# An added zero matmul and copy, and three stores, ahead of the reads of a flag at the end of a one-core attention and maxout kernel

## The chip, the cores and the metric

The kernel runs on one core of a Trainium2 chip. The metric is the device time of one execution in microseconds (us). The five engines of the core (TensorE, VectorE, ScalarE, GpSimd, SyncE) have an instruction stream each and wait for one another through semaphores. In the profile they are PE (with PEld for the loading of weights), DVE, ACT, POOL and SP; a "q" behind the name (SPq, ACTq, DVEq, PEldq) marks instructions that the engine's sequencer handles, such as the issue of a DMA, the load of a register or a branch.

## What is computed

```
scores  = x @ state^T / sqrt(64)           x 8 x 8 x 512 x 64, state 8 x 8 x 32 x 64
xread   = softmax(scores) @ state
sread   = softmax(state @ x^T / sqrt(64)) @ x
y       = concat([xread, sread])           per batch 544 rows of 512 features
h       = max(y @ w1, y @ w2, y @ w3)      512 -> 768
out     = h @ w_out                        768 -> 512, 4352 rows, float32
```

Softmax in the reference subtracts the maximum of each row. The kernel first computes everything without that subtraction and looks at the sums of the exponentials. If all are within bounds, the result stands. If not, everything is computed again with the maximum subtracted.

## The kernel before

The order of the work on every engine is written out by hand, as a list of short words that the kernel performs in turn: FIRST for the batches 0 to 2 and the loading, EACH for a batch in the middle, LAST for batch 7 and for the states' rows of all batches ("s"). Each word is a function in a table: `l2p b j c0 c1` computes columns c0 to c1 of the rows j of a batch's output into a PSUM bank (six accumulating matmuls, line 460), `l2pc` copies that piece to SBUF on the engine named by its last letter (line 464; D for VectorE, A for ScalarE), `sop` stores it from the queue named (line 470, or 468 for rows of the states; S for SyncE, A for ScalarE, P for GpSimd). `l2`, `l2c` and `so` do the same for whole rows of 512 columns (lines 445, 452, 475), `sos` stores a whole row of the states' output (line 483).

PSUM is held as four banks and two pairs of banks. The string BANKS lists, for each bank that the plan asks for in turn, which of the four it gets. The last eight entries before the change are, for the last eight pieces, 2 0 3 1 2 3 0 1; the last of them, bank 1, belongs to `l2p 7 0 128 256`, which VectorE copies and ScalarE stores. The entry before it in the same bank is `l2p s 0 0 256`, which ScalarE copies.

`busy n` (keep_busy) sends n matmuls of a tile of zeros into a bank that nobody reads. FIRST uses it at the start.

The sums are looked at by `look` (VectorE) and turned into a single integer, the flag, by `flag`: one matmul, a reduction and a comparison, lines 502 to 505. `vl` (read_flag, line 510) lets every engine load the flag from SBUF into a register of its own. Each engine then compares the register and branches (line 600): if the flag is zero it jumps over the block that computes everything again. The branch is hinted as likely taken. After the block every engine sets its semaphore to the value that it would have with the block, and SyncE goes through a list of final waits, for all DMA queues and all engines, before the barrier that ends the program. The profile gives these last steps to line 665, that of the call of the kernel.

As every engine's stream is in the order of the words, `vl` stands on each engine behind the work that the list names ahead of it and before what it names later. Before the change `vl` has three words behind it, which are all SyncE's: `sos 1 S`, `sop s 0 0 256 S` and `sop 7 0 256 384 S`. On TensorE and VectorE it is behind the last matmul and the last copy, on ScalarE behind the last store, on GpSimd behind its own last store.

Of the kernel before, what the change touches and what calls it, by code (L numbers as in the profile page):

```python
# [9 lines left out]
F32 = mybir.dt.float32  # L10
BF16 = mybir.dt.bfloat16
# [46 lines left out]
    l2pc 7 3 0 256 D; l2pc s 0 256 512 D; sop s 0 256 512 A; l2pc 7 2 0 128 A; l2p 7 1 128 384;  # L58
    sop 7 2 0 128 A; l2p 7 0 256 384; l2p 7 1 384 512; l2pc s 0 0 256 A; l2p 7 0 128 256;
    l2pc 7 1 128 384 A; l2c s 1 D; sop 7 3 0 256 S; sop 7 2 128 384 P; l2pc 7 0 256 384 D;  # L60
    sop 7 1 128 384 A; l2pc 7 1 384 512 D; sop 7 1 384 512 A; l2pc 7 0 128 256 D; sop 7 0 128 256 A; vl;
    sos 1 S; sop s 0 0 256 S; sop 7 0 256 384 S;
"""

BANKS = """
# [3 lines left out]
"""  # L69
PAIRS = """  # L70
    0110101010 1010101010 1001010010 1001010010 10
# [4 lines left out]
def kernel(  # L76
# [10 lines left out]
    nc = tc.nc  # L87

    B, H, S, D = x.shape
# [16 lines left out]
    work = ctx.enter_context(tc.tile_pool(name="work", bufs=2))  # L106
# [18 lines left out]
    zero = const.tile([128, 512], BF16, name="zero")  # L125
# [17 lines left out]
    def bank(shape, dtype, name):  # L143
        return pp.tile(shape, dtype, tag="b" + next(homes["b"]), bufs=1, name=name)
# [364 lines left out]
    def read_flag():  # L509
# [3 lines left out]

    table = {
        "lst": (load_st, 0), "lx": (load_x, 1), "lxg": (load_x_heads, 1), "lxu": (load_x_uncast, 1),
        "cxu": (cast_x, 1), "lw": (load_w, 0), "lwo": (load_wout, 0), "zero": (set_zero, 0),
# [6 lines left out]
        "gr": (g_run, 1), "grc": (g_ran, 1), "l1": (layer1, 1), "l1s": (layer1_states, 0),  # L525
        "m0": (max_first, 1), "ma": (max_second, 1), "mb": (max_third, 1), "l2": (layer2, 1), "l2c": (layer2_out, 1),
        "l2p": (layer2_part, 1), "l2pc": (layer2_part_out, 1), "sop": (store_part, 1), "so": (store, 1), "sos": (store_states, 0), "look": (look_at_sums, 0), "flag": (set_flag, 0),
        "vl": (read_flag, 0),
    }

    def value(t):
# [138 lines left out]
```

## Time and profile before

| | us |
|---|---|
| median of three runs | 155.25 |
| the three runs | 154.92, 155.25, 155.26 |
| the profiled execution | 154.63 |
| its span, first to last instruction | 152.8 |
| TensorE busy in the span | 146.5 (96%) |
| VectorE busy | 114.4 (75%) |
| ScalarE busy | 85.1 (56%) |
| GpSimd busy | 54.0 (35%) |

The profiled execution's mean granted TensorE clock is 0.994 of full speed. Its own time holds 1.8 us beside the span. Times inside the trace count from the start of the span.

The rows shown below are of these kinds. A row of the chain of waits, or of the timeline, has start, length, engine, line, operation and tiles, with the count of what is merged. A row for one line of the kernel has engine, operation and count, then the shortest, median and longest duration in nanoseconds, then the first and the last start in microseconds. A row of waits names who waited, for whom, and the microseconds in total, the number of waits and the longest. A row of DMA packets names the queue, the number of packets that began in the window, their megabytes, and the time that they took as a share of 16 DMA engines over the window; as a packet counts with its whole length where it began, a short window can hold more than 100%.

### The profile page before, as it was taken

The page shows a single profiled execution, that of the slowest core. Times are in us where ns is not written, and L with a number is a line of the kernel's source. Part 1 is how long each engine was busy: PE and PEld are TensorE (multiplying, and loading weights), DVE is VectorE, ACT ScalarE, POOL GpSimd, SP SyncE. Part 2 cuts the span into 40 slices and gives each one's busy share as a digit, 9 for nine tenths or more (in the row PEclk, how much of TensorE's full clock was granted, in tenths as well). Part 3 has the DMA queues.
Part 4 walks back from the last instruction along what each step waited for, and adds up shares of the span by engine and source line. Part 5 has one row for each costly group of instructions (what it writes and reads, how often), then busy time and mean ns, then how long its engine had stood idle before and what let it go on. Part 6 is the DMA issues. An engine that isn't in the chain of part 4 may idle for free.

```text
span 152.8 us, 3639 instructions
## 1 busy us (share of the span) xinstructions
PE 146.5 (96%) x1433; PEld 73.6 (48%) x1433; DVE 114.4 (75%) x201; ACT 85.1 (56%) x147; POOL 54.0 (35%) x73
## 2 busy tenths in 40 slices
PE   6899999999999999999999999999999999999970
PEld 2465444344445443544354434443444445689660
DVE  1698899889168798879887988898879878664540
ACT  0776876779677762776277627762676362522020
POOL 6978527302246506440644063407140100003300
PEclk9999999999999999999999999999999999999997
DMA  4999999992919979987398839973052300300572
GB/s 110 242 193 202 198 197 203 166 193 41 202 70 241 228 99 271 132 183 178 138 131 183 180 137 133 197 166 137 4 178 54 137 4 2 137 0 21 191 288 66
DMA packets 38053, 22.30 MB, mean 146 GB/s; under 512 B 21504, under 2 KB 35840, under 8 KB 38032
## 3 DMA queue, kind: packets, MB, share of 16 engines
q0 software_dynamic: 14672, 13.44, 45.3%
q1 hardware_dynamic: 21920, 6.95, 22.5%
q10 hardware_dynamic: 1440, 1.64, 3.3%
q8 instruction: 12, 0.20, 0.5%
q14 instruction: 9, 0.07, 0.2%
HBM read 15.20 MB, written 8.91 MB: 158 GB/s over the span
## 4 chain that ended last, share of the span: by engine, by line
PE 92%; ACT 2%; DMA 2%; DVE 1%; issue 0%; ACTq 0%
PE pw L414 47%; PE po L445 25%; PE pg L361 6%; PE po L460 4%; PE ps L260 3%; PE idle L209 2%; PE psr L325 2%; DMA stf<-in_state_dram 2%; PE pgh L361 1%; ACT L226 1%; ACT xT L242 1%; PE pat L293 1%; PE pxt L235 1%; PE pt L220 0%; ACT bd L226 0%; ACT st L215 0%
## 5 line engine op out<-in xcount | busy, mean ns | idle before, releaser
L414 PE MATMUL pw<-aT,G 128*128 128x512 bf16 x288 | 66.6, 379 | 0.0
L429 ACT CAST t<-pw 128x512 bf16<-128x512 f32 (+1 forms) x54 | 30.4, 563 | 35.2 <-PE pw L414 23.1
L414 PEld LDWEIGHTS <-G 128*128 128x128 bf16 x288 | 27.2, 98 | 33.8 <-issue 2.4
L434 DVE TENSOR_TENSOR t<-t,pw 128x512 bf16<-128x512 bf16 (+1 forms) x54 | 35.3, 654 | 10.1 <-ACT t L429 7.6
L445 PE MATMUL po<-wout,ht 128*128 128x512 bf16 x168 | 39.8, 379 | 0.0
L438 DVE TENSOR_TENSOR ht<-t,pw 128x512 bf16<-128x512 bf16 x48 | 32.9, 686 | 4.1
L445 PEld LDWEIGHTS <-ht 128*128 128x128 bf16 x168 | 15.3, 98 | 19.2 <-issue 2.1
L475 POOL DMA_DIRECT2D out_dram<-osb x12 | 6.9, 574 | 49.4 <-ACT t L429 27.2
L282 POOL TENSOR_TENSOR a<-e,rden 128x1024 bf16<-128x1024 bf16 (+1 forms) x9 | 14.8, 1647 | 11.6 <-DVE rden L276 10.5
L401 ACT CAST G<-pg 128x1024 bf16<-128x1024 f32 (+1 forms) x19 | 17.1, 908 | 0.0
L309 POOL COPY xp<-x 128x1024 bf16<-128x1024 bf16 x12 | 12.3, 1065 | 4.8 <-DMA x<-in_x_dram 4.8
L452 DVE COPY osb<-po 128x512 f32<-128x512 f32 x14 | 9.6, 685 | 5.6 <-PE po L445 5.6
L452 ACT COPY osb<-po 128x512 f32<-128x512 f32 x15 | 8.9, 593 | 5.8 <-PE po L445 5.8
L209 PE MATMUL idle<-zero 128*128 128x512 bf16 x30 | 10.2, 440 | 1.3 <-DVE zero L187 1.3
L361 PE MATMUL pg<-w,bd 64*32 64x512 bf16 (+1 forms) x288 | 10.8, 362 | 0.0
L274 DVE TENSOR_REDUCE seen<-e 128x32 f32<-128x1024 bf16 (+1 forms) x10 | 10.0, 998 | 0.5 <-ACT e L267 0.4
L267 ACT ACTIVATE e<-ps 128x1024 bf16<-128x1024 f32 (+1 forms) x10 | 8.6, 861 | 1.6 <-PE ps L260 1.5
L401 DVE CAST G<-pg 128x1024 bf16<-128x1024 f32 (+1 forms) x10 | 9.5, 948 | 0.0
L470 POOL DMA_DIRECT2D out_dram<-osb x4 | 2.1, 540 | 19.9 <-ACT osb L464 19.9
L379 ACT CAST G<-pg 128x768 bf16<-128x768 f32 (+1 forms) x10 | 7.7, 773 | 2.1 <-PE pg L361 2.1
L414 PE MATMUL pw<-atp,w 128*128 128x256 bf16 x72 | 8.7, 272 | 0.0
L414 PEld LDWEIGHTS <-w 128*128 128x128 bf16 x72 | 6.9, 98 | 1.5
(68 smaller groups left out, 112.5 us busy)
## 6 DMA issues: line engine op xcount, KB each, us to landing
out_dram<-osb POOLq DMA_DIRECT2D x11, 512.0 KB, 3.2
x<-in_x_dram POOLq DMA_DIRECT2D x4, 512.0 KB, 7.0
x<-in_x_dram POOLq DMA_DIRECT2D x7, 256.0 KB, 8.7
w<-in_moe_w_dram POOLq DMA_DIRECT2D x3, 384.0 KB, 8.8
w<-in_moe_w_dram POOLq DMA_DIRECT2D x4, 256.0 KB, 8.0
wout<-in_moe_w_out_dram POOLq DMA_DIRECT2D x1, 768.0 KB, 9.9
out_dram<-osb SPq DMA_DIRECT2D x3, 256.0 KB, 2.3
osb<-in_x_dram SPq DMA_DIRECT2D x1, 512.0 KB, 4.2
```

The lines of the kernel that those rows point to most:

```text
L209: nc.tensor.matmul(p, zero[:, 0:128], zero, start=True, stop=True)
L274: nc.vector.reduce_sum(out=den, in_=parity(e[b], g), axis=AX.X)
L282: times[c](out=parity(a[b], g).rearrange("p j g s n -> p j (g s) n"), in0=parity(e[b], g).rearrange("p j g s n -> p j (g s) n"), in1=rdens ...
L309: nc.gpsimd.tensor_copy(out=xp[b][:, :, :, g * (D + 1):g * (D + 1) + D], in_=v[:, g])
L361: nc.tensor.matmul(p(s, g), bd(b, 2 * s + g)[64 * g:64 * g + 64, g, :], f(w_sb[64 * g:64 * g + 64, s]), start=True, stop=True, tile_positi ...
L401: copier[c[g]](out=v[:, g:h], in_=p[:, g:h, 0:c1 - c0])
L414: nc.tensor.matmul(pw[i][:, 0:n], lhs(i, k), rhs(k), start=(k == 0), stop=(k == nk - 1))
L429: nc.scalar.copy(out=t0s[b, m][:, 0:n], in_=open_ps["l", b, m][0][:, 0:n])
L434: nc.vector.tensor_max(t1s[b, m][:, 0:n], t0s.pop((b, m))[:, 0:n], open_ps["l", b, m][1][:, 0:n])
L438: nc.vector.tensor_max(ht[b][:, m, :], t1s.pop((b, m))[:, 0:n], open_ps.pop(("l", b, m))[2][:, 0:n])
L445: nc.tensor.matmul(p, ht[b][:, m, j * 128:(j + 1) * 128], wout_sb[:, m, :], start=(m == 0), stop=(m == NM - 1))
L452: copier[c[i]](out=o[:, j, i * w:i * w + w], in_=p[:, i * w:i * w + w])
```

## The change

A new word, `hold`, sends one matmul of zeros (128 x 128 weights, 512 columns) to one more entry of BANKS, which is bank 1 again, and lets VectorE copy the 128 x 512 result into a new tile, `held`, which nobody reads. `vl` moves behind `hold`, to the end of LAST. So on TensorE the zero matmul stands ahead of the read of the flag, on VectorE the copy, and on SyncE the three stores. ScalarE and GpSimd keep their order.

```diff
@@ LAST
-    sop 7 1 128 384 A; l2pc 7 1 384 512 D; sop 7 1 384 512 A; l2pc 7 0 128 256 D; sop 7 0 128 256 A; vl;
-    sos 1 S; sop s 0 0 256 S; sop 7 0 256 384 S;
+    sop 7 1 128 384 A; l2pc 7 1 384 512 D; sop 7 1 384 512 A; l2pc 7 0 128 256 D; sop 7 0 128 256 A;
+    sos 1 S; sop s 0 0 256 S; sop 7 0 256 384 S; hold; vl;
@@ BANKS, its last line
-    2012301230 1302132103 2130231032 1032130213 0231031031 0321031203 1231031201 3203103203 20312301
+    2012301230 1302132103 2130231032 1032130213 0231031031 0321031203 1231031201 3203103203 203123011
@@
+    def hold_branches():
+        p = bank([128, 512], F32, "idle")
+        nc.tensor.matmul(p, zero[:, 0:128], zero, start=True, stop=True)
+        held = work.tile([128, 512], BF16, tag="held", bufs=1, name="held")
+        nc.vector.tensor_copy(out=held, in_=p)
@@ the table
-        "vl": (read_flag, 0),
+        "vl": (read_flag, 0), "hold": (hold_branches, 0),
```

## The prediction

> **What bounds the kernel now.** I read the page first, then the chain of waits cut to its tail, SyncE's waits, the reads of the flag, the branches behind them, and the DMA packets in narrow windows.
>
> ```profile
> span 152.8 us, 3639 instructions
> ...
> q8 instruction: 12, 0.20, 0.5%
> q14 instruction: 9, 0.07, 0.2%
> ...
> PE 92%; ACT 2%; DMA 2%; DVE 1%; issue 0%; ACTq 0%
> ...
> 145.58 2.66 PE po L460 x36
> 148.24 0.02 issue
> 148.27 0.29 DVE osb L464
> ```
>
> TensorE sets the time up to 148.24 and VectorE's last copy ends at 148.56. Nothing in the change stands ahead of that, so it cannot touch the first 148.6 us. What is left is 4.2 us of stores and final waits. Two DMA queues, q8 and q14, carry instructions.
>
> Next, SyncE's waits after 148 us, then the final waits of line 665 by window (148.8 to 149.5, 149.6 to 152.1, then VectorE's own):
>
> ```profile
> SPq L665 <- DMA out_dram<-osb: 1.8, 1, 1.8
> SPq L665 <- ACTq L510: 0.3, 1, 0.3
> ...
> L665 SPq EVENT_SEMAPHORE  x8: 28/28/300, 148.9 to 149.4; - x8
> ...
> L665 SPq EVENT_SEMAPHORE  x5: 28/28/300, 149.4 to 151.9; - x5
> L665 SPq DRAIN  x2: 7/10/13, 151.9 to 152.0; - x2
> ...
> L665 DVEq DRAIN  x1: 17/17/17, 149.8 to 149.8; - x1
> ```
>
> SyncE goes through a list of final waits, eight in 0.5 us (0.07 us apart), then stands 1.8 us for a store, and its last wait returns at 151.9. From there to the end are 0.9 us that everything has to pass. VectorE was done at 149.8. So a landing store sets the end. The stores' own rows (line 470, windows around each issue; the landing line belongs to the window, and where a window holds two stores its ends are theirs):
>
> ```profile
> L470 ACTq DMA_DIRECT2D out_dram<-osb x1: 339/339/339, 147.7 to 147.7; - x1
> ...
> DMA to landing us min/median/max: 2.0/2.0/2.0
> ...
> L470 SPq DMA_DIRECT2D out_dram<-osb x1: 376/376/376, 147.9 to 147.9; - x1
> ...
> DMA to landing us min/median/max: 2.0/2.8/3.6
> ...
> L470 ACTq DMA_DIRECT2D out_dram<-osb x1: 412/412/412, 148.7 to 148.7; - x1
> ...
> DMA to landing us min/median/max: 3.2/3.2/3.2
> ```
>
> The 128 KB store of 147.7 landed in 2.0 us. The 64 KB one of 147.9 took 3.6 (lands 151.5), and the last one, of 148.7, took 3.2 (lands 151.9): exactly SyncE's last wait. Half the bytes, 1.2 to 1.6 us more. The packets tell why: three windows of 0.02 us around 149.28, 149.66 and 150.28, then all packets from 149 to 149.95 and from 149.95 to 151.5 (shares are of 16 DMA engines):
>
> ```profile
> q8 instruction: 1, 0.02, 397.8%
> ...
> q14 instruction: 1, 0.01, 178.8%
> ...
> q14 instruction: 1, 0.01, 142.2%
> ...
> DMA packets 432, 0.22 MB, mean 235 GB/s; under 512 B 60, under 2 KB 430, under 8 KB 430
> ...
> DMA packets 38, 0.03 MB, mean 21 GB/s; under 512 B 4, under 2 KB 36, under 8 KB 36
> ...
> q10 hardware_dynamic: 27, 0.01, 3.3%
> q1 hardware_dynamic: 9, 0.00, 1.6%
> ```
>
> At 149.28 one instruction packet of 0.02 MB begins; 3.978 x 16 x 0.02 us = 1.27 us on one DMA engine. At 149.66 a smaller one takes 1.788 x 16 x 0.02 = 0.57 us, at 150.28 another 0.46 us. By 149.95 the stores are done but for 36 packets. A 64 KB store is 128 rows over 16 engines, 8 packets and one under 512 B on each; 36 packets with 4 small ones are four such shares, left behind on one or two engines. That these are the engines with the instruction packets is inferred (the trace does not number engines), but nothing else runs there. **The kernel waits some 1.2 us at its end for pieces of stores queued behind fetched instructions.** Whose they are, the branches tell (line 510 is the read of the flag, line 600 the branch and what follows):
>
> ```profile
> L510 SPq TENSOR_LOAD <-flag x1: 772/772/772, 145.1 to 145.1; - x1
> L510 PEldq TENSOR_LOAD <-flag x1: 490/490/490, 147.1 to 147.1; - x1
> L510 DVEq TENSOR_LOAD <-flag x1: 736/736/736, 148.3 to 148.3; - x1
> L510 ACTq TENSOR_LOAD <-flag x1: 484/484/484, 149.1 to 149.1; - x1
> ...
> L600 PEldq COMPARE_BRANCH  x1: 390/390/390, 147.7 to 147.7; - x1
> L600 PEldq EVENT_SEMAPHORE  x1: 51/51/51, 148.3 to 148.3; - x1
> L600 SPq COMPARE_BRANCH  x1: 64/64/64, 148.3 to 148.3; - x1
> L600 DVEq COMPARE_BRANCH  x1: 84/84/84, 149.1 to 149.1; - x1
> L600 DVEq EVENT_SEMAPHORE  x1: 21/21/21, 149.7 to 149.7; - x1
> ```
>
> Branch to fetch: TensorE 147.7 to 149.28, 1.6 us; SyncE 148.3 to 149.66, 1.4; VectorE 149.1 to 150.28, 1.2. TensorE's is the large one and comes just as the last stores move.
>
> **The change part by part.** The timeline rows that price it:
>
> ```profile
> 144.12 1.46 PE L445 MATMUL po<-wout,hts 128*128 128x512 bf16 x6
> ...
> 145.62 0.69 DVE L452 COPY osb<-po 128x512 f32<-128x512 f32 x1 [0.59 <-PE po L445]
> 146.71 0.37 ACT L464 COPY osb<-po 128x256 f32<-128x256 f32 x1 [0.50 <-PE po L460]
> 147.92 0.38 SPq L470 DMA_DIRECT2D out_dram<-osb  x1
> ...
> L209 PE MATMUL idle<-zero x30: 376/379/634, 1.3 to 15.4; 128*128 128x512 bf16 x30
> ```
>
> *TensorE.* The zero matmul writes the bank of piece 0, columns 128 to 256, and waits for its copy, 148.56; say it starts at 148.6. Behind it on TensorE stand only the read and the branch. Does the read wait too? Before, the last piece's matmuls waited for the bank of the states' first half, whose ACT copy ends 146.71 + 0.37 = 147.08, and the read starts at 147.1 although matmuls ran on to 148.2: it goes when the last waiting matmul is released. So now it starts at 148.6, the branch 0.6 later at 149.2, the fetch 1.6 later at 150.8 (1.2 by VectorE's gap: 150.4). Both are behind 149.95, where undisturbed stores have no packets left.
>
> The Trainium skill, page "Perfetto Trace Analysis", section "Tensor Engine Instruction (MATMUL, LD_WEIGHTS)", says the sequencer pushes an instruction into a wait queue and goes on to the next, the wait being served in the queue. By that rule the read would pass the waiting matmul and nothing would move (a rival below); the 147.1 row speaks against it.
>
> *VectorE.* The matmul is read 145.62 - (144.12 + 1.46 - 0.38) = 0.42 us after its start (by L209 between 0.38 and 0.63; I take 0.42, TensorE having just worked), so the copy starts at 149.0. VectorE's old read began at 148.3 with the last copy (148.27), not at its end; so now 149.0, branch 0.8 later at 149.8, next instruction 0.6 later at 150.4, done 150.5. If the read waits for the copy's end, add 0.69 (the L452 copy; half the bytes written, so no more). Nobody waits for the held tile itself, but SyncE's final list waits for VectorE's count. VectorE's fetch moves to 151.0, after the stores.
>
> *SyncE.* Its three stores (lines 483, 468, 470) are no longer behind the read; that brings nothing, since the old read was over at 145.9, ahead of the first store's data (145.62 + 0.69 = 146.31). The read now stands behind the last one: 147.92 + 0.38 = 148.3, plus 0.77, branch 149.1, first final wait 0.6 later at 149.7 instead of 148.9. Thirteen waits 0.07 apart end at 150.6. This 0.8 us is covered by the landing stores; without that cover it would be lost whole. SyncE's fetch moves from 149.66 to some 150.5, also off the stores.
>
> *ScalarE and GpSimd* read as before; ScalarE's read (149.1) still follows its last store's issue.
>
> *The stores.* With the fetches gone, 148.7 + 2.0 (the 147.7 store's landing) = 150.7.
>
> *The sum.* Last wait: the latest of 150.7 (store), 150.6 (SyncE's list), about 150.6 (VectorE's 150.4 and two waits behind it) = 150.7 against 151.9: **1.2 us less**, span 151.6. The profiled execution took 154.63, 1.8 around its span; it would take 153.4. It lies 0.6 under the median of the runs, so I take the difference to the median: 155.25 - 1.2 = 154.05. Three arms end within 0.1 us of each other, so a faster store alone gains hardly more: 1.3 by the list, 153.95, less 0.25 for the spread of single runs, 153.7.
>
> **The rivals.** *VectorE takes the place of the stores*: its read waits for the copy's end (+0.69) and perhaps the matmul is slow (+0.21): its part ends at 151.3, or 151.5, gain 0.4 to 0.6: about 154.75. For it: its arm is already level with the store's. Against: the old read's start.
>
> *It doesn't do what it says*: the read passes the waiting matmul, or another late fetch (VectorE's, ScalarE's) falls on the same pieces: 155.2. Against: the 147.1 row; for: a wait so close ahead of a read is seen twice only. Here also falls a fetch that the end now has to wait for: TensorE's at 150.8 plus 1.27 is over at 152.1, past my last wait, and if its final instructions lie in that page the gain is eaten.
>
> *Slower*: the page of the branch's target isn't there when the branch is taken. One matmul and one copy shift the code behind them, and the branch now comes when the sequencer has nothing left to cover a fetch. Price at TensorE: branch 149.2, fetch at 150.8, 1.27 of transfer, 0.6 to the next instruction: 152.7, two waits more 152.8, 0.9 later than today: 156.1. It decides once branch to next instruction exceeds some 2.6 us (then the last wait is past 151.9). Against: today it is 0.6 us on TensorE, SyncE and VectorE, and each fetch comes after that next instruction, so the target was there already.
>
> The Trainium skill, page "Runtime: NRT & Kernel Launch", section "Instruction fetch mechanics", states that a taken branch whose target lies outside the two pages held forces a fetch before execution goes on. By it every branch here would stall, as in this rival; the trace does not show that stall in the kernel before.
>
> **How the numbers follow.** Forecast 0.62 (own range 153.7 to 154.6), VectorE's arm 0.10, no effect 0.15, slower 0.13. A measurement of this kernel can tell about 0.3%, 0.47 us: faster means under 154.78, so the first two count as faster, 0.72; the third as the same, 0.15; the fourth as slower, 0.13. The range 153.7 to 155.4 takes in all but the fourth.
>
> **What would show it.** Right: TensorE's read at 148.6 instead of 147.1; the 16 KB packet at 150.4 or later; no store packets after about 150; the last three stores landing in 1.7 to 2.2 us; SyncE's last wait at 150.6 to 150.8, without 1.8 us on a store. VectorE's rival: SyncE's longest wait names VectorE. No effect: the large packet still at 149.3. Slower: more than 2 us between branch and next instruction, with a q8 packet in between. The prediction is wrong if the stores land late with no instruction packet near them, or if the change moves the first 148.6 us.

## The result and the profile after

| | before | changed |
|---|---|---|
| median, us | 155.15 (6 runs) | 153.34 (6 runs) |
| lowest and highest | 154.76, 155.56 | 153.16, 154.13 |
| profiled execution | 154.63 | 153.68 |
| its span | 152.8 | 151.8 |

The ratio is 0.989, with a 95% interval of 0.987 to 0.992: faster by 1.2 to 2.1 us. The forecast was 154.05 in 153.7 to 155.4. The direction and the mechanism held; the time lies 0.36 us below the range.

Of the changed kernel first the tail of the timeline of VectorE and of TensorE (start, length), then the reads (line 510, as before) and the branches (line 606 now), with first and last start in us:

```profile
148.00 0.96 DVE L464 COPY osb<-po 128x128 f32<-128x128 f32 x3 [1.29 <-PE po L460]
149.43 0.69 DVE L520 CAST held<-idle 128x512 bf16<-128x512 f32 x1 [0.47 <-PE idle L518]
...
149.02 0.38 PE L518 MATMUL idle<-zero 128*128 128x512 bf16 x1 [0.38 <-DVE osb L464]
...
L510 SPq TENSOR_LOAD <-flag x1: 662/662/662, 148.8 to 148.8; - x1
L510 PEldq TENSOR_LOAD <-flag x1: 577/577/577, 149.0 to 149.0; - x1
L510 DVEq TENSOR_LOAD <-flag x1: 546/546/546, 149.4 to 149.4; - x1
...
L606 PEldq COMPARE_BRANCH  x1: 385/385/385, 149.7 to 149.7; - x1
L606 DVEq COMPARE_BRANCH  x1: 84/84/84, 150.1 to 150.1; - x1
L606 DVEq EVENT_SEMAPHORE  x1: 21/21/21, 150.6 to 150.6; - x1
```

Everything ahead of the change is 0.4 us later in this execution than in the profiled one of before: VectorE's three copies end at 148.96 here and at 148.56 there. So the ends must be compared from a common point. I take L, the start of VectorE's last copy of a piece (the end of those three copies less 0.29): 148.27 before, 148.67 here. From L to the end of the span, the tail, it was 4.6 us before and is 3.1 here. The reads of TensorE and VectorE have moved behind the zero matmul's wait (149.0) and behind the start of the held copy (149.4).

Next the last stores' rows (the landing line of a window holds for the stores in it), the packets from 150.81 to 150.83 and from 150.35 to 151.7, and SyncE's waits after 148:

```profile
L470 ACTq DMA_DIRECT2D out_dram<-osb x1: 338/338/338, 148.1 to 148.1; - x1
L470 SPq DMA_DIRECT2D out_dram<-osb x1: 383/383/383, 148.3 to 148.3; - x1
...
DMA to landing us min/median/max: 1.9/1.9/1.9
...
L470 ACTq DMA_DIRECT2D out_dram<-osb x2: 338/372/406, 148.7 to 149.1; - x2
...
DMA to landing us min/median/max: 1.7/1.7/1.7
...
q8 instruction: 1, 0.02, 452.5%
...
DMA packets 4, 0.04 MB, mean 30 GB/s; under 512 B 0, under 2 KB 0, under 8 KB 0
...
q8 instruction: 1, 0.02, 6.7%
q14 instruction: 3, 0.02, 6.5%
...
SPq L671 <- PEq L671: 0.7, 2, 0.5
SPq L468 <- ACT osb L464: 0.6, 1, 0.6
```

The three stores that took 3.2 to 3.6 us land in 1.7 to 1.9. The large instruction packet begins at 150.81, 2.14 us after L instead of 1.01, and takes 4.525 x 16 x 0.02 = 1.45 us. It ends at L + 3.59, behind the end of the span (L + 3.11), so nothing at the end waits for it. From 150.35 on no packet of a store is left: the four that begin there are all instructions. SyncE's wait of 1.8 us on a store is gone. Its last waits:

```profile
L671 SPq EVENT_SEMAPHORE  x9: 28/28/28, 150.0 to 150.6; - x9
...
L671 SPq EVENT_SEMAPHORE  x4: 28/28/76, 150.6 to 150.8; - x4
L671 SPq DRAIN  x2: 7/10/13, 150.9 to 150.9; - x2
```

They begin at 150.0, 1.36 us after L, and end at 150.8, when the last store lands (149.1 + 1.7). The store still sets the end, by very little.

### The profile page after: what moved, and what is told of

Read it like the earlier page. It is cut to its first block, busy times and chain, and to the rows that moved or that the text cites. A ratio compares the mean times of both kernels' runs of the same rounds, so it can differ in the third digit from the quotient of the medians.

```text
span 151.8 us, 3628 instructions
## 1 busy us (share of the span) xinstructions
PE 146.3 (96%) x1420; PEld 73.6 (48%) x1434; DVE 115.2 (76%) x202; ACT 85.3 (56%) x147; POOL 54.0 (36%) x73
## 4 chain that ended last, share of the span: by engine, by line
PE 87%; DMA 7%; POOL 3%; issue 2%; DVE 1%; POOLq 0%
PE pw L414 47%; PE po L445 25%; DMA w<-in_moe_w_dram 7%; PE pg L361 6%; PE po L460 4%; PE ps L260 2%; POOL w L179 2%; PE psr L325 2%; POOL x L168 1%; PE pgh L361 1%; DVE held L520 0%; PE pt L220 0%; PE idle L518 0%; DVE osb L464 0%; POOL ident masks.py:199 0%
## 5 line engine op out<-in xcount | busy, mean ns | idle before, releaser
L445 PE MATMUL po<-wout,ht 128*128 128x512 bf16 x155 | 39.1, 380 | 0.7
```

Source lines behind the costliest of these rows:

```text
L445: nc.tensor.matmul(p, ht[b][:, m, j * 128:(j + 1) * 128], wout_sb[:, m, :], start=(m == 0), stop=(m == NM - 1))
```

## The experiments

Each ratio is to the kernel before on the same chip. L, the tail and the last landing come from one profiled execution each.

| | L | span | tail | last landing after L | ratio, 95% interval |
|---|---|---|---|---|---|
| before | 148.27 | 152.8 | 4.6 | 3.58 | 1 |
| e1, before again | 148.39 | 152.7 | 4.4 | 3.37 | 0.999, 0.996 to 1.001 |
| e2, SyncE's stores ahead | 148.68 | 153.3 | 4.6 | 3.64 | 1.000, 0.998 to 1.002 |
| e3, matmul and copy alone | 148.18 | 151.7 | 3.5 | 2.55 | 0.994, 0.991 to 0.996 |
| e4, without the copy | 148.08 | 151.2 | 3.1 | 2.12 | 0.989, 0.986 to 0.992 |
| the change | 148.67 | 151.8 | 3.1 | 2.12 | 0.989, 0.987 to 0.992 |
| e9, the change again | 148.20 | 151.3 | 3.1 | 2.12 | 0.989, 0.985 to 0.993 |
| e5, in bank 0 | 148.30 | 151.4 | 3.1 | 2.11 | 0.991, 0.989 to 0.994 |
| e6, in bank 2 | 149.32 | 154.0 | 4.7 | 3.69 | 1.001, 0.999 to 1.004 |
| e7, two in a row | 148.05 | 152.3 | 4.2 | 2.09 | 0.998, 0.995 to 1.000 |
| e8, no branch at all | 148.04 | 151.1 | 3.0 | 2.10 | 0.991, 0.989 to 0.994 |

**e1, the kernel before again.** No edit.

> The kernel before, unchanged, for a second trace and more times. Ratio 1.000. If the late stores of the first trace are the rule: the 16 KB instruction packet again begins about 1.6 us behind TensorE's branch, the last store lands 3 us or more after its issue, and from the start of VectorE's last copy to the end of the span there are 4.5 us (4.57 in the first trace, 3.11 in the changed kernel's). If that trace was an odd one: a landing near 2 us and 3.5 us or less to the end. The start of the last copy tells how much the work ahead of the change varies (148.27 before, 148.67 in the changed kernel's trace).

```profile
SPq L665 <- DMA out_dram<-osb: 1.6, 1, 1.6
...
L470 ACTq DMA_DIRECT2D out_dram<-osb x1: 408/408/408, 148.8 to 148.8; - x1
...
DMA to landing us min/median/max: 3.0/3.0/3.0
```

The late stores are the rule: 3.0 us for the last one, 1.6 us of SyncE's waiting, a tail of 4.4 us. The large packet began 1.01 us after L again.

**e2, only SyncE's stores ahead of the reads.**

```diff
-    sos 1 S; sop s 0 0 256 S; sop 7 0 256 384 S; hold; vl;
+    sos 1 S; sop s 0 0 256 S; sop 7 0 256 384 S; vl;
```

> Only SyncE's stores stand ahead of the reads; no zero matmul, no copy. Theory (TensorE's fetch holds the stores): TensorE reads and branches where it did, its packet begins near 149.3, the last three stores still land after 3 us or more, ratio 1.000 within 0.003. Rival (moving SyncE's read is what helped): ratio 0.990.

```profile
L510 PEldq TENSOR_LOAD <-flag x1: 491/491/491, 147.6 to 147.6; - x1
...
q8 instruction: 1, 0.02, 367.2%
...
SPq L671 <- DMA out_dram<-osb: 1.4, 1, 1.4
```

TensorE reads 1.1 us before L as it did, the large packet (1.18 us) begins in the window around 149.70, and SyncE still waits 1.4 us for a store. Alone, SyncE's part brings nothing.

**e3, the zero matmul and the copy alone.**

```diff
-    sos 1 S; sop s 0 0 256 S; sop 7 0 256 384 S; hold; vl;
+    hold; vl;
+    sos 1 S; sop s 0 0 256 S; sop 7 0 256 384 S;
```

> The zero matmul and the copy alone; SyncE reads ahead of its three stores as before. Theory: the large packet moves behind the stores, but SyncE's 0.57 us packet stays near 149.7 (taken to the same start) and holds one share of the last store by some 0.5 us: the gain is the changed kernel's less 0.4 to 0.5 us, ratio 0.992 to 0.994. Rival (SyncE's part helps): ratio 1.000. Rival (SyncE's part is nothing): 0.989, like the change.

```profile
q14 instruction: 1, 0.01, 359.4%
...
L470 ACTq DMA_DIRECT2D out_dram<-osb x1: 412/412/412, 148.6 to 148.6; - x1
...
DMA to landing us min/median/max: 2.1/2.1/2.1
...
SPq L671 <- DMA out_dram<-osb: 0.5, 1, 0.5
```

The large packet is behind the stores, but at 149.575 a small one begins (3.594 x 16 x 0.01 = 0.57 us) and the last store lands in 2.1 us instead of 1.7. The tail is 0.4 us longer than the change's. So SyncE's part, worth nothing alone, is worth 0.4 us once TensorE's packet is out of the way: then its own packet is the one that holds the last store.

**e4, the zero matmul without VectorE's copy.**

```diff
-        held = work.tile([128, 512], BF16, tag="held", bufs=1, name="held")
-        nc.vector.tensor_copy(out=held, in_=p)
```

> The zero matmul without VectorE's copy; SyncE's stores ahead. VectorE reads and branches where it did, its packet begins near 150.3. Theory (TensorE's packet is nearly all): ratio 0.989 as the change, 0.2 us less at most since VectorE's part of the end is no longer level with the stores. Rival (VectorE's read is what matters): near 1.000.

```profile
L510 DVEq TENSOR_LOAD <-flag x1: 734/734/734, 148.1 to 148.1; - x1
...
L510 PEldq TENSOR_LOAD <-flag x1: 567/567/567, 148.4 to 148.4; - x1
...
DMA to landing us min/median/max: 1.7/1.7/1.7
...
q8 instruction: 1, 0.02, 402.5%
```

The last row is of the packets from 150.20 to 150.22: the large one begins there, at L + 2.12 as in the change. VectorE reads at L as before, and yet the last store lands in 1.7 us and the tail is 3.1. The copy in the change does nothing for the time.

**e5 and e6, the zero matmul in a bank that comes free earlier.** The last entry of BANKS is 0, then 2, in place of 1.

```diff
-    2012301230 1302132103 2130231032 1032130213 0231031031 0321031203 1231031201 3203103203 203123011
+    2012301230 1302132103 2130231032 1032130213 0231031031 0321031203 1231031201 3203103203 203123010
```

> The change with the zero matmul in bank 0, whose piece (columns 384 to 512 of row 1) VectorE copies one copy earlier; times are taken from the start L of VectorE's last copy of a piece. The zero matmul is then released at about L instead of L + 0.3. Theory (the read goes when the last waiting matmul ahead of it is released, the packet follows the branch): TensorE's read at L + 0.05, branch at L + 0.7, the 16 KB packet at L + 1.8 (1.1 behind the branch as in the last three traces) to L + 2.2. The last store's packets are over by L + 1.7, so all the gain stays: last landing near L + 2.1, ratio 0.989. Rival (the matmul must wait for the last piece to help): ratio above 0.993.

> The zero matmul in bank 2, whose piece (columns 128 to 384 of row 1) ScalarE copies, ending near L - 0.6. Theory: read at L - 0.6, branch near L + 0.1, the packet at L + 1.2 to L + 1.65, in the packets of the last store alone, so that store's last share lands near L + 3.1 (3.58 in the kernel before, 2.12 with the change), the two stores ahead of it land in about 2 us: gain 0.4 to 0.6 us, ratio 0.996. Rival (any zero matmul there brings the gain, or the sequencer runs past it): 0.989, or 1.000.

Of e6, the reads, the packets around 150.85 and from 151.1 to 153, and the landing of the two stores before the last and of the last:

```profile
L510 PEldq TENSOR_LOAD <-flag x1: 658/658/658, 148.7 to 148.7; - x1
...
q8 instruction: 1, 0.02, 337.5%
...
q10 hardware_dynamic: 9, 0.00, 2.3%
...
DMA to landing us min/median/max: 1.7/1.8/1.9
...
DMA to landing us min/median/max: 3.3/3.3/3.3
```

Bank 2: the read goes at L - 0.6, the large packet begins at L + 1.53 and takes 1.08 us. The two stores before the last land in 1.7 to 1.9 us, as expected. The last one takes 3.3: nine of its packets, the share of one DMA engine, are left after 151.1. I had expected half of the gain to stay; none did. With one share behind the large packet the last store lands at L + 3.69, with three, in the kernel before, at L + 3.58. Two things made up for the smaller load. The large packet itself ended later, at L + 2.61 against L + 2.29. And the nine packets began there, at L + 2.59, and took 0.53 us together, while the 27 of the three shares took 0.83; another instruction packet was under way from L + 2.53 to L + 3.10, but that it slowed them is not shown. In both kernels the last packet of a store ends at about L + 3.1.

Of e5, the packets from 150.76 to 150.77:

```profile
q8 instruction: 1, 0.02, 596.9%
```

Bank 0: the read goes 0.34 us earlier than with bank 1, at L, and the packet begins at L + 2.46, behind the stores: the same tail as the change. That packet came 1.6 us after its branch, where 1.1 was expected; either way it is past L + 1.7. The pair answers the question of whether TensorE's read passes a waiting matmul: it goes when the zero matmul's bank is free, in all three banks.

**e7, two zero matmuls with their copies.**

```diff
-    sos 1 S; sop s 0 0 256 S; sop 7 0 256 384 S; hold; vl;
+    sos 1 S; sop s 0 0 256 S; sop 7 0 256 384 S; hold; hold; vl;
@@ BANKS, its last entry
-203123011
+2031230111
```

> Two zero matmuls, each with its copy, both in bank 1, so that the second matmul waits for the first copy. Theory (the parts of the end are nearly level, so a later read comes straight off the gain): VectorE's second copy and its read at L + 1.9, its branch at L + 2.55, its count complete at L + 3.15, SyncE's last wait at L + 3.3 instead of L + 2.14, named VectorE: 1.1 to 1.2 us of the gain are lost, ratio 0.996 to 0.997. Rival (what comes after the stores costs nothing): 0.989.

```profile
149.97 0.69 DVE L520 CAST held<-idle 128x512 bf16<-128x512 f32 x1 [0.47 <-PE idle L518]
...
L510 DVEq TENSOR_LOAD <-flag x1: 546/546/546, 150.0 to 150.0; - x1
...
SPq L671 <- DVEq L510: 0.8, 1, 0.8
SPq L671 <- DVEq L606: 0.5, 1, 0.5
```

The stores land as early as with the change, but SyncE now waits 0.8 and 0.5 us for VectorE's read and count. The tail grows by 1.1 us. So the delay of the reads has an upper limit, and the change's single matmul is close to it.

**e8, no branch.** This kernel leaves out the reads of the flag, the branch and the block that computes everything again; on this input that block is jumped over.

```diff
-    sop 7 1 128 384 A; l2pc 7 1 384 512 D; sop 7 1 384 512 A; l2pc 7 0 128 256 D; sop 7 0 128 256 A; vl;
+    sop 7 1 128 384 A; l2pc 7 1 384 512 D; sop 7 1 384 512 A; l2pc 7 0 128 256 D; sop 7 0 128 256 A;
...
-    with tc.If(bad != 0, label="again"):
...
```

> The kernel before without the reads of the flag, the branches and the block that computes everything again with the maximum subtracted; the flag is still computed. Theory: with no branch there is no instruction packet after 148 us, the last store lands near L + 2.1, SyncE's last wait follows it, and the tail from L to the end of the span is 3.1 us as in the changed kernel: ratio 0.989, so the change has taken away all that the branches cost at the end. Rival (the reads and branches themselves also cost): a tail under 2.9 us, ratio 0.987 or less.

Of its DMA packets from 148 to the end all the queues, and of its issues ScalarE's two and SyncE's one:

```profile
q10 hardware_dynamic: 432, 0.26, 26.6%
q1 hardware_dynamic: 322, 0.23, 22.7%
...
out_dram<-osb ACTq DMA_DIRECT2D x2, 64.0 KB, 1.7
out_dram<-osb SPq DMA_DIRECT2D x1, 64.0 KB, 1.9
```

With no instruction packet in that time the stores land in the same 1.7 and 1.9 us as with the change, and the tail is 3.0 us. The change has taken away all but 0.1 us of what the branches cost at the end.

**e9, the change again.**

> The change as it is, for a second trace and a narrower ratio. If the tail (from L, the start of VectorE's last copy, to the end of the span) is the whole of it: tail 3.1 us again against 4.4 to 4.6 without the change, last landing at L + 2.1, and a ratio of 1 - 1.41/154.8 = 0.991, within 0.989 to 0.993. If the change also shortens what comes ahead of L: a ratio under 0.989.

Tail 3.1 us, last landing at L + 2.12, L itself at 148.20. The ratio is 0.989 but its interval, 0.985 to 0.993, holds 0.991 as well.

## Why the prediction was right or wrong

**Right: what sets the end.** Pieces of the last stores waited behind instructions fetched after the branches, TensorE's 16 KB packet above all. e2 (packet unmoved, nothing gained), e4 (packet moved by the matmul alone, all gained), e6 (packet moved into the last store alone, nothing gained) and e8 (no packets, no late stores) show it. That a packet and the late shares are on the same DMA engine remains an inference, as the trace does not number the engines, but a close one: in all five traces with late shares (before, e1, e2, e3, e6) these begin within 0.02 us of the end of an instruction packet. In the kernel before, nine begin at 150.23, where SyncE's packet ends (149.66 + 0.57), and the first of 27 at 150.55, where TensorE's ends (149.28 + 1.27). In e2, where SyncE's packet came later, only 27 are left.

**Right: where the reads go.** TensorE's was put at 0.3 us after L and stands there; VectorE's at 0.7, measured 0.8, with the start of the held copy and not with its end, so the rival in which VectorE takes the place of the stores did not come. The rule that a waiting matmul doesn't hold back what is behind it, which would have made the change idle, does not hold for these reads (e5, e6). The branch's target was there each time (0.44 to 0.57 us from the branch to the next instruction in the change), so the slower rival did not come.

**Wrong: the size, in two steps.** The first is the sum's own term for the last store. I gave it the 2.0 us of the 128 KB store issued at 147.7; the stores at the end are of 64 KB, and undisturbed the last one lands in 1.7 us (the change, e4, e5, e8, e9). The other two arms were too long as well: SyncE's list ends by L + 2.1 and not 2.3, as it starts 1.36 and not 1.43 us after L and its waits are 0.06 apart, and VectorE's read took 0.55 us, not 0.74. In the sum the tail of the changed kernel was 3.3 us; it is 3.1. Against 4.4 to 4.6 in the three traces with an undisturbed TensorE read (before, e1, e2; mean 4.5) that makes 1.4 us, where the prediction had 1.2 and, by SyncE's list, at most 1.3. In the profiled execution that was read, the tail's difference is 4.57 - 3.11 = 1.46.

The second is the step "I take the difference to the median". The median of the three runs shown, 155.25, was high. Beside the experiments the kernel before took 154.76 (29 runs), 154.82 (24 runs) and 154.86 (11 runs). The six runs of the result itself, which hold those three, have 155.15; why this set is slower is open. Of the 0.71 us between forecast and measurement, 0.4 to 0.5 come from the starting point, against these later medians, and 0.2 to 0.3 from the sum. Both go the same way, and the lower end lay only 0.35 us under the forecast. Reckoned from the profiled 154.63, the same 1.2 us would have given 153.43, near the measured 153.34, but by luck: that execution was some 0.2 us faster than the medians, which makes up for the gain put too small.

The tail's 1.4 us are 0.9% of the time. The ratios' intervals of the change and of e9, 0.985 to 0.993 together, hold that; a ratio of 0.989 would be 1.7 us. The traces show no gain ahead of L that would explain the rest. TensorE's first matmuls of line 414 (layer one), before and then changed, the latter with the row ahead of them:

```profile
16.80 1.47 PE L414 MATMUL pw<-aT,G 128*128 128x512 bf16 x6
...
16.74 0.52 PE L361 MATMUL pg<-w,bd 64*32 64x384 bf16 x16 [0.58 <-DMA w<-in_moe_w_dram]
17.19 1.47 PE L414 MATMUL pw<-aT,G 128*128 128x512 bf16 x6
```

From the start of line 414 to L there are 131.47 us before and 131.48 with the change, so the change shortens nothing in between. The 0.4 us by which the changed execution runs late arose ahead of it, where TensorE waits 0.58 us for weights. Ten of the eleven traces have 131.45 to 131.48 us here; e6 has 132.29, and its further 0.8 us arose between 34 and 49 us. The last 79.1 us ahead of L are the same to 0.01 us in all eleven. L scatters from 148.04 to 149.32, with and without the change, because of what comes earlier, and that is more than the 0.3 us in question.

**Costs put at nothing.** SyncE's later read is covered by the landing stores, as said, and the held copy is unread and unneeded (e4). That SyncE's fetch also moves off the stores was said but not priced by itself; once TensorE's is out of the way, it is worth 0.4 us (e3). That the parts of the end are nearly level, so that a further delay comes straight off, was right: e7 lost 1.1 us of the 1.4.

## What to carry to other kernels

In this kernel the branches at the end cost more than their own instructions. The fetch behind TensorE's branch was one packet of 0.96 to 1.45 us, and the last store, which lands in 1.7 us undisturbed, took 3.0 to 3.3 us with a share of it behind that packet. Compare the landing times of equal stores; when the last ones take longer than earlier ones, look for instruction packets in that window, and try to hold the branch until the data has gone, but not past its landing. Delaying work that nothing depends on was a gain here, and the delay has a best length: too short, the packet still meets the last store (e6); too long, the end waits for the branch (e7).

## What was unexpected

- One share of one store behind the large packet was enough to lose the whole gain (e6: landing at L + 3.69; before, with three shares: L + 3.58). In e6 the packet also ended 0.32 us later.
- The late shares begin just where an instruction packet ends, to 0.02 us, SyncE's small packet included.
- The large packet begins 1.5 us after TensorE's branch in the kernel before, e1 and e2, 1.1 us in the change, e3, e4, e7 and e9, 1.35 us in e6 and 1.6 us in e5. What sets this gap was not tried.
- The same read of the flag took 0.74 us on VectorE in the kernel before and 0.55 with the change, 0.77 and 0.66 on SyncE, 0.49 and 0.58 on TensorE.
- The start of VectorE's last copy differs by 0.6 us between executions of kernels whose work ahead of it is the same (148.04 to 148.68), and was 149.32 in one of them, although the last 79.1 us ahead of it are the same in all: single executions are compared from a point inside them, not from their start.
